# TensorE in a hardware loop of four packs, 16 heads' weights at a time, and V in 2 KB rows: two attention blocks on one core

**Chip, cores, metric.** One core of a Trainium2 chip. The metric is the device time of one execution in microseconds, lower is better. The four runs of the kernel before lie within 0.3% of each other (823.37 to 825.63 us).

## The reference

Two independent blocks A and B, the outputs joined along the last axis:

```python
B, Sq, D = 16, 64, 640          # batches, queries, width
H, Sk, Dh = 32, 512, 128        # heads, keys, head width
q = (x @ wq).reshape(B, Sq, H, Dh).transpose(0, 2, 1, 3)
scores = einsum("bhqd,bhkd->bhqk", q, k_cache) * Dh ** -0.5
p = softmax(scores, axis=-1)
o = einsum("bhqk,bhkd->bhqd", p, v_cache)
out = o.transpose(0, 2, 1, 3).reshape(B, Sq, H * Dh) @ wo      # all bf16
```

K and V are 67 MB each per block; about 292 MB must be loaded in all.

## The kernel before

The unit of work is a *pack*: four heads of two batches (2 x 64 queries fill the 128 rows). There are 128 packs. A planner lists the operations of every engine in order, finds which semaphores each must wait for, and the emitter writes all of it out, one instruction after the other. Per pack:

- TensorE: Q projection QP (20 matmuls), scores S (32 matmuls in 32x64 tiles), transposes of the normalised weights TR (2 x 8), PV (2 x 16), output projection OP (8). Each matmul comes with a weight load, so two instructions.
- VectorE: transposes K (KT, twice 1.24 us), evicts Q (QE) and the transposes (TE), reciprocals (RC).
- ScalarE: four exponentials (EX), two evictions of PV (OE). GpSimd: four normalisations (NM), and the reordering of a 512-column piece of wq (WP, 2.5 us) when a block begins.
- SyncE: all loads, in a planned order, into rings of buffers.

The parts that the change touches:

```python
def em_LDV(e, op):                    # V: 1 KB per descriptor
    src = blocks[blk][2][2 * bp + b, 4 * j:4 * j + 4].rearrange("g (p t) d -> p g t d", p=128)
    ...
def em_PV(e, op):                     # per pair of heads
    for s in range(2):
        for b in range(2):
            for t in range(4):
                col = s * 128 + 64 * b
                last = e.matmul(o_ps[:, col:col + 64], v_ring[:, n % NV, b, 2 * a + s, t, :],
                                pT_ring[:, m % NT, s, t, 64 * b:64 * b + 64], start=(t == 0), stop=(t == 3))
def em_OP(e, op):                     # per pair of heads; summed in PSUM over all 32 heads
    for s in range(2):
        h = (2 * m + s) % H
        last = e.matmul(out_ps0, oT_ring[:, m % NO, s, :], wo_sb[:, h, 0:N0], start=(h == 0), stop=(h == H - 1))
        ...                           # and the last 128 of 640 columns into out_ps1
def run_program(e, eng, p):
    for op in progs[eng]:             # every engine, TensorE too, is written out
        ...                           # waits, the instructions, the semaphore increment
```

## Time and profile before

| | before |
|---|---|
| time, median of 4 runs | 824.13 us |
| first scores / start of pack 8 / scores of the last pack | 12.1 / 91.1 / 805.9 us |
| mean pack from pack 8 on | 6.007 us |
| shortest pack | 5.30 us |
| 16 KB packets on the instruction queue | 112 |
| load rate in the steady stretches | 375 GB/s |

The lines of the page, of the two steady windows, of one hole and of the start stand in the prediction. A "pack" in the table is the time from one pack's first score matmul to the next one's. From pack 8 to the end the time is 119 x 6.007 us plus a tail, so whatever changes the mean pack by 0.1 us changes the total by 12 us.

### The profile page before, as it was taken

What the parts mean: (1) busy time and instruction counts of PE and PEld (TensorE: products, weight loads), DVE (VectorE), ACT (ScalarE), POOL (GpSimd) and SP (SyncE); (2) the same over time, 40 slices, a digit from 0 to 9 for tenths busy, and PEclk for the clock granted to TensorE, in tenths of its full rate; (3) what the DMA queues carried; (4) which work ended last, traced back from release to release, by engine and by line L of the source; (5) the groups of instructions that cost most, each with busy time, mean ns of one, the idle gap of its engine ahead of it and who ended that gap; (6) DMA issues with size and microseconds to landing.
All of it is one profiled execution on the core that took longest, in us unless ns stands there. A gap on an engine that the chain in (4) does not pass through costs nothing.

```text
span 824.6 us, 31476 instructions
## 1 busy us (share of the span) xinstructions
PE 707.0 (86%) x13777; PEld 521.7 (63%) x13905; DVE 578.7 (70%) x902; ACT 419.6 (51%) x1313; POOL 388.2 (47%) x550
## 2 busy tenths in 40 slices
PE   3069999999999999998778989999999999999994
PEld 2046776767666767676556666666666666666773
DVE  3047787777777787777556767777777777787773
ACT  2025655555554645554444555555555464555552
POOL 2068444444444444445665444444454444454442
PEclk9999999999999999999999999999999999999997
DMA  9999999999999999999999999999999999999980
GB/s 329 364 372 367 377 378 376 378 373 379 373 374 376 371 380 375 373 375 370 339 319 377 372 378 377 376 376 376 376 375 373 377 373 376 375 374 376 377 284 13
DMA packets 195729, 296.79 MB, mean 360 GB/s; under 512 B 9216, under 2 KB 162816, under 8 KB 195584
## 3 DMA queue, kind: packets, MB, share of 16 engines
q1 hardware_dynamic: 193280, 292.06, 100.2%
q8 instruction: 112, 1.84, 0.9%
q10 hardware_dynamic: 2304, 2.62, 0.9%
q14 instruction: 33, 0.27, 0.1%
HBM read 292.03 MB, written 2.62 MB: 357 GB/s over the span
## 4 chain that ended last, share of the span: by engine, by line
PE 70%; DMA 10%; SPq 6%; issue 6%; POOL 5%; DVE 3%; ACT 0%; ACTq 0%
PE ps L380 15%; PE ps L403 14%; PE ps L462 14%; PE ps L446 12%; PE ps L476 9%; DMA v_ring<-in_B_v_cache_dram 8%; PE ps L479 5%; DMA ws_ring<-in_A_wq_dram 2%; SPq L349 2%; SPq L342 2%; DVE kt_ring L393 2%; POOL pn_ring L438 2%; POOL wqp_sb L356 1%; POOL wqp_sb L357 1%; SPq L335 1%
## 5 line engine op out<-in xcount | busy, mean ns | idle before, releaser
L438 POOL TENSOR_SCALAR pn_ring<-p_ring,recip 128x512 bf16<-128x512 bf16 x512 | 349.2, 694 | 382.0 <-DVE recip L433 382.0
L418 ACT ACTIVATE p_ring<-ps 128x512 bf16<-128x512 f32 x512 | 304.2, 597 | 262.2 <-PE ps L403 262.2
L393 DVE STREAM_TRANSPOSE kt_ring<-kn_ring 128x1024 f32<-128x1024 f32 x256 | 316.0, 1235 | 7.6 <-DMA kn_ring<-in_A_k_cache_dram 7.5
L451 DVE COPY pT_ring<-ps 128x1024 bf16<-128x1024 bf16 x256 | 177.1, 692 | 161.3 <-PE ps L446 161.3
L446 PE MATMUL ps<-ident,pn_ring 128*128 128x128 bf16 x2048 | 158.0, 220 | 48.0 <-POOL pn_ring L438 46.8
L462 PEld LDWEIGHTS ps<-pT_ring,v_ring 128*128 128x128 bf16 x4096 | 141.5, 98 | 80.1 <-issue 64.7
L462 PE MATMUL ps<-pT_ring,v_ring 128*128 128x64 bf16 x4096 | 168.6, 194 | 21.8 <-issue 11.4
L380 PE MATMUL ps<-xT_ring,wqp_sb 128*128 128x128 bf16 x2560 | 169.7, 222 | 11.4 <-issue 9.1
L403 PE MATMUL ps<-kt_ring,qs_ring 32*64 32x512 bf16 x4096 | 155.2, 398 | 15.5 <-issue 13.4
L446 PEld LDWEIGHTS ps<-ident,pn_ring 128*128 128x128 bf16 x2048 | 122.4, 98 | 64.3 <-POOL pn_ring L438 49.1
L380 PEld LDWEIGHTS ps<-xT_ring,wqp_sb 128*128 128x128 bf16 x2560 | 153.1, 114 | 14.7 <-issue 11.4
L468 ACT ACTIVATE oT_ring<-ps 128x256 bf16<-128x256 f32 x256 | 98.5, 385 | 117.6 <-PE ps L462 117.4
L476 PE MATMUL ps<-wo_sb,oT_ring 128*128 128x512 bf16 x384 | 132.9, 387 | 0.1
L386 DVE TENSOR_SCALAR qs_ring<-ps 128x512 bf16<-128x512 f32 x128 | 88.6, 692 | 60.7 <-PE ps L380 60.7
L479 PE MATMUL ps<-wo_sb,oT_ring 128*128 128x128 bf16 x512 | 113.0, 221 | 8.2 <-issue 1.7
L418 ACT ACTIVATION_READ_ACCUMULATOR p_ring<-ps 128x1 f32 x512 | 105.6, 206 | 0.0
L403 PEld LDWEIGHTS ps<-kt_ring,qs_ring 32*64 32x64 bf16 x4096 | 57.1, 104 | 63.1 <-issue 24.4
L476 PEld LDWEIGHTS ps<-wo_sb,oT_ring 128*128 128x128 bf16 x512 | 50.3, 98 | 65.6 <-ACT oT_ring L468 33.3
L479 PEld LDWEIGHTS ps<-wo_sb,oT_ring 128*128 128x128 bf16 x512 | 50.7, 99 | 0.2 <-issue 0.2
L433 DVE RECIPROCAL recip<-rowsum 128x2 f32<-128x2 f32 x256 | 36.3, 142 | 6.6 <-ACT p_ring L418 6.4
L356 POOL COPY wqp_sb<-ws_ring 128x1280 bf16<-128x1280 bf16 x16 | 20.0, 1253 | 41.4 <-DMA ws_ring<-in_A_wq_dram 41.4
L357 POOL COPY wqp_sb<-ws_ring 128x1280 bf16<-128x1280 bf16 x16 | 20.1, 1256 | 0.0
(19 smaller groups left out, 39.5 us busy)
## 6 DMA issues: line engine op xcount, KB each, us to landing
kn_ring<-in_A_k_cache_dram SPq DMA_DIRECT2D x128, 512.0 KB, 10.2
v_ring<-in_A_v_cache_dram SPq DMA_DIRECT2D x128, 512.0 KB, 10.7
kn_ring<-in_B_k_cache_dram SPq DMA_DIRECT2D x128, 512.0 KB, 10.2
v_ring<-in_B_v_cache_dram SPq DMA_DIRECT2D x128, 512.0 KB, 10.7
ws_ring<-in_A_wq_dram SPq DMA_DIRECT2D x8, 640.0 KB, 9.4
wo_sb<-in_A_wo_dram SPq DMA_DIRECT2D x8, 640.0 KB, 10.6
ws_ring<-in_B_wq_dram SPq DMA_DIRECT2D x8, 640.0 KB, 8.3
wo_sb<-in_B_wo_dram SPq DMA_DIRECT2D x8, 640.0 KB, 11.2
```

Of the source, the lines that this page charges most:

```text
L380: last = e.matmul(ps[:, 0, f * 128:(f + 1) * 128], w[:, kt, f, :], xT_ring[:, xs, kt, :], start=(kt == 0), stop=(kt == KT - 1))
L386: ins = e.tensor_scalar(qs_ring[:, op.idx % NQ].rearrange("p f b q -> p (f b q)"), ps[:, 0, :], scale, None, ALU.mult)
L393: ins = e.transpose(dst, kn_ring[:, n % NK, b, :].bitcast(F32))
L403: last = e.matmul(ps[64 * b:64 * b + 64, i, :], qs_ring[rows, n % NQ, f, b, :], kt_ring[rows, n % NKT, b, :, f // 2, :, f % 2], start=(f = ...
L418: ins = e.activation(dst, src, ACTF.Exp, scale=1.0, accum_out=rowsum[:, h:h + 1])
L438: ins = e.tensor_scalar(pn_ring[:, h % NPN, :], p_ring[:, h % NP, :], recip[:, (h // 2) % NR, h % 2:h % 2 + 1], 1.0, ALU.mult, ALU.mult)
L446: last = e.transpose(pt_ps[:, s, t, :], pn_ring[:, h % NPN, t * 128:(t + 1) * 128], ident[:, :])
L451: ins = e.tensor_copy(pT_ring[:, op.idx % NT].rearrange("p s t q -> p (s t q)"), pt_flat)
L462: last = e.matmul(o_ps[:, col:col + 64], v_ring[:, n % NV, b, 2 * a + s, t, :], pT_ring[:, m % NT, s, t, 64 * b:64 * b + 64], start=(t == ...
L468: ins = e.activation(oT_ring[:, op.idx % NO].rearrange("p s q -> p (s q)"), o_ps, ACTF.Copy)
L476: last = e.matmul(out_ps0, oT_ring[:, m % NO, s, :], wo_sb[:, h, 0:N0], start=(h == 0), stop=(h == H - 1))
L479: last = e.matmul(out_ps1, oT_ring[:, m % NO, s, :], wo_sb[:, h, N0:D], start=(h == 0), stop=(h == H - 1))
```

## The change

Its intent: TensorE's program is turned into a hardware loop, so that its instructions need not be fetched again and again. A *turn* is one pass through the loop body. The body is written once, so its addresses and wait values are the same in every pass. So buffers and weights must repeat with the body (NJ = PERIOD = NV = 4 packs, thus 16 heads' weights in SBUF at a time instead of 32), the output sums of the two halves of the heads are added in SBUF, and every semaphore that TensorE waits for is lowered at the end of a turn by what a turn added. V comes in rows of 2 KB; a partition then holds eight keys in a row, a head takes 64 partitions, and PV becomes pairs of matmuls over half the rows, in two row tiles of the array.

```diff
-    NK = 5   NV = 5   NWS = 2   NP = 4   NPN = 4   NO = 2          (condensed)
+    NK = 7   NV = 4   NWS = 4   NP = 2   NPN = 2   NO = 1   PERIOD = 4   FIRST = 3
-            src = blocks[blk][2][2 * bp + b, 4 * j:4 * j + 4].rearrange("g (p t) d -> p g t d", p=128)
+            src = blocks[blk][2][2 * bp + b, h:h + 4].rearrange("(a s) (p t) d -> (s p) a (t d)", s=2, t=8)
@@ em_PV: once a pack
-            for s in range(2):
+            for a in range(2):
                 for b in range(2):
-                    for t in range(4):
-                        last = e.matmul(o_ps[:, col:col + 64], v_ring[:, n % NV, b, 2 * a + s, t, :], ...)
+                    for t in range(8):
+                        for s in range(2):
+                            rows = slice(64 * s, 64 * s + 64)
+                            last = e.matmul(o_ps[:, s, col:col + 64], v_ring[rows, n % NV, b, a, t, :],
+                                            pT_ring[rows, (2 * n + a) % NT, t, 64 * b:64 * b + 64],
+                                            start=(t == 0), stop=(t == 7), tile_position=(64 * s, 0))
@@ em_OP: once a pack, a pack later; new em_OA, em_OV add the sums into acc on VectorE
@@ run_program, for TensorE
+            with e.Fori(0, reps):
+                for op in prog[lo:lo + size]:
+                    emit(e, op, p, {})
+                for s, v in sorted(per.items(), key=str):
+                    e.sem_inc(sems[p][s], -v * units(s))
```

Cut: the planner's checks that the waits are periodic, the replacement of waits that would not be, new order times, and the exponential's and the transposes' addressing.

## The prediction

> **What bounds the kernel now.** I read the page first, then the windows by stage, then the order of time inside single packs, then the waits, and last the trace's packet records. A pack is four heads of two batches: 1 MB of K, 1 MB of V; there are 128 of them. From the page:

> ```profile
> span 824.6 us, 31476 instructions
> PE 707.0 (86%) x13777; PEld 521.7 (63%) x13905; DVE 578.7 (70%) x902; ACT 419.6 (51%) x1313; POOL 388.2 (47%) x550
> ...
> PE   3069999999999999998778989999999999999994
> ...
> DMA  9999999999999999999999999999999999999980
> GB/s 329 364 372 367 377 378 376 378 373 379 373 374 376 371 380 375 373 375 370 339 319 377 372 378 377 376 376 376 376 375 373 377 373 376 375 374 376 377 284 13
> ...
> q1 hardware_dynamic: 193280, 292.06, 100.2%
> q8 instruction: 112, 1.84, 0.9%
> ```

> Two things are full at once. TensorE is at 9 in nearly every slice, except the first three and slices 19 to 23, where new weights come in. The DMA engines are at 9 from the first slice to the 38th, and their rate never passes 380 GB/s. The windows of the two steady stretches say the same (columns: length, busy time of PE, PEld, DVE, ACT, POOL with counts, clock, DMA share, GB/s):

> ```profile
> 110.00:390.00 280.00, 259.60 (x5121) 192.09 (x5165) 214.65 (x334) 156.28 (x492) 131.93 (x192) 1.00 1.06 375
> 444.00:780.00 336.00, 307.56 (x6102) 227.21 (x6155) 255.04 (x397) 184.68 (x580) 154.06 (x226) 1.00 1.06 375
> ```

> Which leads? Taking pack starts (first score matmul of each pack) from the trace, a pack lasts 5.31 us when nothing disturbs TensorE, and that exact value comes back again and again (packs 12, 30, 36, 48, 51, 108). The mean between packs 66 and 120 is (767.0 - 444.7) / 54 = 5.97 us. The difference is holes like this one (PE rows in order of time; the bracket is idle time and what ended it):

> ```profile
> 239.09 0.72 PE L380 MATMUL ps<-xT_ring,wqp_sb 128*128 128x128 bf16 x10
> 241.19 0.75 PE L380 MATMUL ps<-xT_ring,wqp_sb 128*128 128x128 bf16 x10 [1.38 <-issue]
> ```

> The hole splits one run of identical matmuls, so no data is missing: the instructions are. The queue of instruction fetches has 112 packets of 16 KB, one for every 256 TensorE instructions, and one starts at 238.71 us, just before this hole. So **instruction fetch** costs TensorE some 0.5 to 0.6 us a pack. Behind it stands the DMA. V of packs 72 to 84 lands within 0.1 us of its first use; by pack 126 it is 7.6 us early. The loads thus gain only about 7.6 / 42 = 0.18 us a pack on TensorE: DMA-limited period about 5.75 us, TensorE about 5.95.

> The start is lost too. From the chain of waits:

> ```profile
> 35.49 9.42 DMA ws_ring<-in_A_wq_dram
> 44.96 1.26 POOL wqp_sb L356
> 46.22 1.20 POOL wqp_sb L357
> ```

> TensorE starts at 12 us, then waits until 49 us for a slice of wq that sits in the queue behind 30 us of other loads, because the two staging slots had to come free first.

> [...]whether a loop stays resident no run here shows yet. [...]packets of 1,024 bytes take 49.6 ns, of 4,096 bytes 168.5 ns, not four times as much. [...]Here scores (32x64 tiles) issue matmuls 3 to 4 ns apart in groups of eight, and the change from transposes to scores costs 149 ns start to start instead of 56, that from scores to PV 314 instead of 213: some 95 ns each.

> **The change, part by part.**

> *TensorE per pack, from 5.31 us.* Scores (1.07), transposes (8 at 56 ns, twice, 0.90) and the Q projection (20 at 56 ns, 1.12) stay. PV had 32 matmuls at 29 ns, 0.94 us; now it has 64 with half the rows, two row tiles at a time. If two tiles run side by side, as the scores do, 32 pairs at 29 ns are 0.94 us again. PV now needs a tiling mode of its own: two more mode changes, +0.19. The output projection had 4 x (0.215 + 0.056) = 1.08 us plus a wait of 0.265 us for the second head pair's eviction (321 ns start to start where 56 would do; "ACT oT_ring L468" ends 33.3 us of such waits). It now starts a pack later on one eviction for all four heads: -0.265. Sum 5.24 us.

> *Instruction fetch.* The loop body is 4 x (20 + 32 + 16 + 64 + 8) + 5 = 565 matmuls, two instructions each, 1,130, with waits and a dozen semaphore decrements about 1,150[...]. The choice of 16 heads, which makes addresses repeat after four packs, only makes sense if this fits; eight packs would be 2,260. I take it that it stays resident: the 0.6 us holes go[...]. TensorE period about 5.4 us. 31 turns of the loop: 124 x 0.5 = 62 us off TensorE's path.

> *DMA.* Sum of packet times over 16 engines before: 1,024-byte packets 141,312 x 49.6 ns / 16 = 438 us, 1,280-byte loads 38, 4,096-byte 345, stores 7, instructions 8, semaphores and tables 7: 842 us in a window of about 798 us (the page's 1.06: packets overlap a little). A line through the two sizes gives 2,048 bytes 89.2 ns. V's 131,072 packets become 65,536: 406 -> 365 us, -41. Instruction fetch falls by about 7. x is loaded once more for each half of the heads, +2,048 packets of 1,280 bytes, +7.6. New sum 801, times 798/842: 760 us. If the overlap is a constant 3.9 ns per packet instead, a V packet of each size loses that, V gives only 25 us, and the window is 773. I take 765. This is what the change is worth per pack: 5.75 -> about 5.5.

> *Other engines.* VectorE gets the partial sums[...]. ScalarE loses 16 output copies and does one eviction of 512 in place of two of 256. GpSimd's weight copies are the same 32 at 1.25 us, now four up front and four at each of three changes; with them a pack needs 2.5 + 4 x 0.694 = 5.3 us of GpSimd, close to the period, where eight packs before took 7.6 us each.

> *Start and end.* Four staging slots and only four wq slices: all are requested before anything can block them, so the stop until 49 us shrinks to a few us. This gives TensorE about 30 us, but it gives the DMA nothing, since that worked through the stop at 364 to 372 GB/s.

> So TensorE needs about 15 + 128 x 5.4 + 10 for changes of weights + 15 = 730 us, the DMA 2 + 765 + the work after the last V. Before, 22 us passed after it because TensorE lagged; now PV, eviction, output projection, sum, store and the closing check remain, estimate 13 us. **The bound moves from TensorE with its instruction fetch to the DMA: 2 + 765 + 13 = 780 us, 5.3% less.**

> **Rivals.**
> 1. *The loop does not stay resident.* Then 1,150 instructions are 4.5 fetches in four packs (1.1 a pack against 0.85), plus a stall of some 3 us at each turn (the last two fetches of the trace, around the closing jump, are 3.1 us apart). TensorE: 5.24 + 0.65 + 0.75 = 6.6 us a pack, total about 880.[...]
> 2. *The row tiles do not overlap.* 64 matmuls at 29 ns are 1.88 us; period about 6.3 us, 31 + 128 x 6.3 = about 835. For it: weight loads of 128 columns come 29 ns apart, no closer, in the PV of now. Against it: the scores' loads go 3 to 4 ns apart in different tiles. At a half-way cost the DMA would still hide it.
> 3. *A chain of latencies sets the period.* Scores, four exponentials and one eviction (about 3.9 us), reciprocal, two normalisations (1.4), transpose: about 6.6 us from a pack's scores to its second transpose, which stands only one pack later in TensorE's order. It closes at about 5.4 us a pack, so it hides under the DMA; with VectorE's added work in the way it could make 5.8: 790.
> 4. *2 KB rows bring nothing*, if the memory and not the packet overhead sets 376 GB/s. Then the DMA stays at 798: total 812, within 2%.

> **Range and chances.** With a resident loop, tilings that overlap and a saturated DMA, the two readings of the overlap give 775 to 788; a better ordered start and end or a larger effect of the packet size allow 757, a latency chain or rival 4 up to 812. I put 10% on rivals 1 and 2 together. Faster by over 2% (below 807): 0.85; within: 0.07; slower: 0.08.

> **What would show it.** Right: the instruction queue falls from 112 packets to about 20; "issue" disappears from TensorE's waits inside packs; DMA share stays at 9 throughout, now at 388 to 395 GB/s; 2,048-byte packets near 89 ns; V lands just before use, and waits for V and K become TensorE's and VectorE's largest. PV about 1 us a pack with gaps of about 0.1 us around it. Wrong: instruction packets over 100, holes of microseconds every four packs, PV matmuls 29 ns apart without pairs, or a DMA below 9 in steady packs, which would put the bound on a chain of engines.

That the body of about 1,150 instructions stays resident was an assumption. One term of TensorE's sum is cut, an estimate for the decrements and the branch at the turn; with it the sum came to about 5.4 us a pack and 730 us in all. The two durations and the sum for VectorE's new work are cut too (it came to 81% busy); in the changed kernel an addition of 128x128 takes 0.28 us, one of 128x512 0.67 us, and VectorE is busy for 78%. The 780 us are the DMA's sum, 2 + 765 + 13, and lose no term. The 13 us for the end and the 10 us for changes of weights are estimates.

## The result

792.4 us (median of 4 runs, 791.67 to 792.93) against 824.13. The ratio is 0.9612 [0.9594, 0.963]. Here and below a ratio is the mean time of one kernel's fast runs over that of the other's fast runs of the same rounds, so not quite the ratio of the medians.

The page of the changed kernel, its lines that answer to those of before:

```profile
span 790.7 us, 40216 instructions
PE 706.0 (89%) x17953; PEld 533.3 (67%) x18081; DVE 616.3 (78%) x1062; ACT 406.8 (51%) x1185; POOL 386.8 (49%) x550
...
PE   4668999999999999999999999999999999999994
...
DMA  9999999999999999999999999999999999999950
GB/s 319 388 396 397 396 393 396 393 394 384 396 385 397 391 377 393 390 388 370 382 392 393 398 397 397 398 396 390 383 389 387 396 399 397 400 398 399 399 215 15
...
q8 instruction: 11, 0.18, 0.1%
```

112 instruction packets became 11, and none of them lies between 74.3 and 774.4 us: the loop stays resident. The loads run up to 400 GB/s. The dips of slices 19 to 24 in TensorE's row are gone. But both rows are still full, and the page does not say which of the two leads. The waits do, all that are over 10 us and end idle time of TensorE (engine, line, what it waited for: total us, times, longest us):

```profile
PEld ps L562 <- PEq L724: 45.3, 31, 1.5
PEld ps L604 <- DVE pT_ring L610: 42.6, 95, 1.5
PE ps L562 <- PEq L724: 39.9, 31, 1.3
PEld ps L522 <- issue: 30.0, 32, 10.8
PE ps L522 <- DMA xn_ring<-in_A_x_dram: 16.4, 2, 10.3
```

There is no line for V or K. The second line is idle time of the weight loads alone, and the matmul row of the same instructions has 1.3 us: scores were running. "PEq" is TensorE's own sequencer and L724 is the row of semaphore decrements at the end of the loop body. 31 turns wait there for 39.9 us. In order of time, TensorE's rows around one turn:

```profile
117.08 1.11 PE L622 MATMUL ps<-pT_ring,v_ring 64*128 64x64 bf16 x64
118.12 0.62 PE L604 MATMUL ps<-ident,pn_ring 128*128 128x128 bf16 x8
120.02 1.14 PE L562 MATMUL ps<-kt_ring,qs_ring 32*64 32x512 bf16 x32 [1.28 <-PEq L724]
```

The trace's own records show why: the twelve decrements start 0.151 us apart, 1.81 us in all, then 0.10 us for the loop counter and 0.27 us for the branch (its record lasts 212 ns). The transposes queued before them cover only part of that.

So from pack 8 on TensorE never waits for loaded data. The packs repeat in fours: 5.41, 5.41, 6.77 (the turn), 5.70 us (the pack with the five transposes of x). The mean is 5.41 + (1.36 + 0.28) / 4 = 5.82 us, and 5.824 is what the starts give. V lands at least 2.0 us ahead of its use in every pack from 9 on. K's lead is below 0.3 us only in packs 101 to 103, after the last change of weights, and no pack there is longer than its fellows.

Where the 33.9 us of the two spans went:

| stretch | before | after | difference |
|---|---|---|---|
| to the start of pack 8 | 91.1 | 79.1 | -12.0 |
| 119 packs to the last | 119 x 6.007 = 714.8 | 119 x 5.824 = 693.1 | -21.8 |
| after the last pack's first scores | 18.6 | 18.5 | -0.1 |

The differences are those of the unrounded times. The middle line is a difference of larger terms. Gone are the fetch holes (714.8 less 119 x 5.31, less about 14 us at the change of block and 4 us of x transposes: about 65 us, of which 8 us were waits for V, over 103 fetches) and the slow change of block. Added are 30 turns at 1.36 us (41 us), 0.10 us a pack (12 us) and twice as many x transposes (4 us).

### The profile page after: what moved, and what is told of

Its sections match the earlier page's. It is cut to its first block, busy times and chain, and to the rows that moved or that the text cites. A ratio compares the mean times of both kernels' runs of the same rounds, so it can differ in the third digit from the quotient of the medians.

```text
span 790.7 us, 40216 instructions
## 1 busy us (share of the span) xinstructions
PE 706.0 (89%) x17953; PEld 533.3 (67%) x18081; DVE 616.3 (78%) x1062; ACT 406.8 (51%) x1185; POOL 386.8 (49%) x550
## 4 chain that ended last, share of the span: by engine, by line
PE 60%; PEld 14%; issue 10%; DVE 8%; SPq 4%; DMA 1%; PEldq 1%; ACT 0%; DVEq 0%
PE ps L562 13%; PE ps L604 12%; PE ps L539 11%; PE ps L622 11%; PE ps L638 8%; PE ps L641 5%; PEld ps L539 5%; PEld ps L622 4%; PEld ps L604 3%; DVE pT_ring L610 3%; SPq L501 2%; DVE kt_ring L552 2%; PE ps L522 2%; DMA xn_ring<-in_A_x_dram 1%; PEld ps L638 1%
## 5 line engine op out<-in xcount | busy, mean ns | idle before, releaser
L577 ACT ACTIVATE p_ring<-ps 128x512 bf16<-128x512 f32 x512 | 298.9, 599 | 189.2 <-PE ps L562 189.2
L610 DVE COPY pT_ring<-ps 128x1024 bf16<-128x1024 bf16 x256 | 173.2, 677 | 118.4 <-PE ps L604 117.8
L562 PE MATMUL ps<-kt_ring,qs_ring 32*64 32x512 bf16 x4096 | 147.1, 398 | 46.5 <-PEq L724 39.9
L629 ACT ACTIVATE oT_ring<-ps 128x512 bf16<-128x512 f32 x128 | 76.4, 597 | 170.5 <-PE ps L622 170.5
L604 PEld LDWEIGHTS ps<-ident,pn_ring 128*128 128x128 bf16 x2048 | 117.3, 98 | 50.5 <-DVE pT_ring L610 42.6
L622 PE MATMUL ps<-pT_ring,v_ring 64*128 64x64 bf16 x8192 | 142.3, 190 | 2.9 <-issue 2.2
L622 PEld LDWEIGHTS ps<-pT_ring,v_ring 64*128 64x128 bf16 x8192 | 126.8, 95 | 15.1 <-issue 2.5
L638 PE MATMUL ps<-wo_sb,oT_ring 128*128 128x512 bf16 x384 | 118.8, 381 | 0.0
L651 DVE TENSOR_TENSOR acc<-acc,ps 128x128 f32<-128x128 f32 x96 | 27.0, 281 | 10.9 <-PE ps L641 2.1
L528 ACT ACTIVATE xT_ring<-ps 128x640 bf16<-128x640 bf16 x32 | 22.3, 696 | 15.0 <-PE ps L522 15.0
```

The costliest lines, as they stand in the source:

```text
L562: last = e.matmul(ps[64 * b:64 * b + 64, i, :], qs_ring[rows, n % NQ, f, b, :], kt_ring[rows, n % NKT, b, :, f // 2, :, f % 2], start=(f = ...
L577: ins = e.activation(dst, src, ACTF.Exp, scale=1.0, accum_out=rowsum[:, h:h + 1])
L604: last = e.transpose(pt_ps[:, t, :], pn_ring[:, op.idx % NPN, t].rearrange("q s k -> q (s k)"), ident[:, :])
L610: ins = e.tensor_copy(pT_ring[:, op.idx % NT].rearrange("p t q -> p (t q)"), pt_flat)
L622: last = e.matmul(o_ps[:, s, col:col + 64], v_ring[rows, n % NV, b, a, t, :], pT_ring[rows, (2 * n + a) % NT, t, 64 * b:64 * b + 64], star ...
L629: ins = e.activation(oT_ring[:, op.idx % NO].rearrange("p s a q -> p s (a q)"), o_ps, ACTF.Copy)
```

## The experiments

**Theory:** the changed kernel is bound by TensorE, through the row of decrements at the turn, with the DMA some ten microseconds behind; the loop pays because its body stays resident. **Rivals:** the DMA already sets the time; or it is the branch that costs.

Ten kernels ran in three batches, each timed in three rounds against the kernel before (medians 825.1, 824.5 and 825.9 us). All gave correct results.

**1. Decrements spread over the body.**

```diff
+            last = {s: i for i, op in enumerate(body) for s, _ in op.waits}
             with e.Fori(0, reps):
-                for op in prog[lo:lo + size]:
+                for i, op in enumerate(body):
                     emit(e, op, p, {})
-                for s, v in sorted(per.items(), key=str):
-                    e.sem_inc(sems[p][s], -v * units(s))
+                    for s, v in sorted(per.items(), key=str):
+                        if last[s] == i:
+                            e.sem_inc(sems[p][s], -v * units(s))
```

> The same loop with its twelve semaphore decrements no longer in one row at the end, but each straight after the last wait of the loop body that uses its semaphore. Theory (the decrements cost 0.151 us each in TensorE's sequencer and, standing together, outlast the queued matmuls): the fourth pack start of each turn falls from 6.77 us to 5.4 to 5.8 us, the idle time put down to TensorE's sequencer at the loop's end falls from 39.9 us to under 12 us, and TensorE's path gets 31 to 42 us shorter. Then the DMA becomes the bound at 297.8 MB / 396 GB/s = 752 us plus about 20 us of start and end: total 768 to 778 us. Rival (the turn's 1.35 us are the branch and the drain of the queue, whatever stands before it): the fourth pack stays at 6.6 to 6.8 us and the total at 788 to 793 us.

Measured 781.52 us, ratio 0.9478 [0.944, 0.9516], the fastest kernel of this study. The turn is gone: the median pack with the turn lasts 5.42 us. But the mean pack is 5.740 us, not 5.48, because now data are missing. The views of waits, changed kernel and then this one (the eviction of Q, `qs_ring`, follows the transposes of K in VectorE's order, so a late K shows at TensorE as a wait for it):

```profile
DVE kt_ring L552 <- DMA kn_ring<-in_A_k_cache_dram: 15.8, 4, 10.1
```

```profile
DVE kt_ring L552 <- DMA kn_ring<-in_B_k_cache_dram: 33.0, 31, 3.4
PEld ps L562 <- DVE qs_ring L545: 31.7, 22, 3.2
...
DVE kt_ring L552 <- DMA kn_ring<-in_A_k_cache_dram: 19.4, 10, 10.0
```

K lands less than 0.3 us before its use in about 60 packs from 9 on. The loss isn't spread evenly: packs 53 to 68 and 91 to 101, around which new weights are loaded beside K and V, take 29 of the 31 us by which the 119 packs exceed TensorE's own 5.41 and 5.69 us; the others run at TensorE's pace. The loads themselves never pause until their end (DMA share 1.04 to 1.05 in the stretches from 80 to 700 us), so TensorE paces ordinary packs and the sum of the loads sets the total. The 41 us taken off TensorE's path brought 11: the DMA took over. Its floor is about 781 us, a little over the 768 to 778 that I expected. The branch as the cause has fallen.

**2. Twelve more decrements.**

```diff
+                for _ in range(6):
+                    e.sem_inc(s_fl, 1)
+                    e.sem_inc(s_fl, -1)
```

> The changed kernel with twelve more semaphore operations at the end of the loop body, on a semaphore that nobody waits for (six times plus one, minus one). Theory (each costs 0.151 us in the sequencer, nothing hides these): a turn gets 12 x 0.151 = 1.81 us longer, the fourth pack 8.5 to 8.7 us, the total 31 x 1.81 = 56 us longer, 843 to 850 us. Rival (branch and drain cost, the decrements are free): total 790 to 800 us.

Measured 883.71 us, 91 us longer, not 56. The pack with the turn lasts 8.63 us, 1.86 longer than 6.77: the theory's 1.81 for each turn. The other 35 us have another cause. The next pack lasts 5.70 us in some turns and 7.3 in others. TensorE's rows around a turn of the second kind, first the output projection before it, then the turn, then the output projection after it:

```profile
410.97 0.38 PE L638 MATMUL ps<-wo_sb,oT_ring 128*128 128x512 bf16 x1
411.19 0.22 PE L641 MATMUL ps<-wo_sb,oT_ring 128*128 128x128 bf16 x1
...
418.05 1.13 PE L562 MATMUL ps<-kt_ring,qs_ring 32*64 32x512 bf16 x32 [3.12 <-issue]
...
420.11 0.63 PE L638 MATMUL ps<-wo_sb,oT_ring 128*128 128x512 bf16 x1
420.54 0.31 PE L641 MATMUL ps<-wo_sb,oT_ring 128*128 128x128 bf16 x1
```

After the hole of 3.1 us the same matmul takes 0.63 us in place of 0.38. The trace's clock records hold 20 windows of 3.413 us at half speed between 129 and 843 us, and one of twice that length at 75 us; the changed kernel has none between 51 and 788 us. 22 x 3.413 / 2 = 38 us at most; the mean granted clock is 0.946 against the changed kernel's 0.987. With 31 x 1.81 = 56 that makes 94, against 91 measured. So most of these holes of 3.1 us cost clock as well as their own length. Some shorter holes did too. In the kernel before, around the window at 395.6 us:

```profile
389.59 0.38 PE L476 MATMUL ps<-wo_sb,oT_ring 128*128 128x512 bf16 x1
...
394.20 0.62 PE L446 MATMUL ps<-ident,pn_ring 128*128 128x128 bf16 x8 [2.09 <-POOL pn_ring L438]
...
397.34 0.63 PE L476 MATMUL ps<-wo_sb,oT_ring 128*128 128x512 bf16 x1
```

The hole of 2.1 us at 430 us there has such a window after it too (at 433.1 us), and five holes of 1.9 to 2.4 us in experiment 5; others of that length have none, such as those of 2.1 us that end at 409.7 and 417.3 us in the kernel before. The changed kernel's turns, with holes of up to 1.3 us, never do.

**3. TensorE written out, the rest as changed.**

```diff
-            if eng != "pe":
+            if True:
                 for op in prog:
                     emit(e, op, p, {})
                 return
```

> The changed kernel without the loop: TensorE's program written out, all else the same. Theory (instruction fetch was the first thing on the path, and the loop is what removed it): 141 or more instruction packets of 16 KB instead of 11, holes put down to issue of 0.5 to 0.7 us each are back, the loop's 42 us are saved; total 815 to 840 us, slower than the changed kernel. Rival (the kernel before was bound by the DMA, its holes were hidden, and the loop brings nothing): total 765 to 792 us.

Measured 880.16 us, ratio 1.0693 to the kernel before, with these packets on the instruction queue:

```profile
q8 instruction: 144, 2.36, 1.1%
```

The loop is worth 88 us here. The total lies outside both expectations, since the holes were longer than I thought: the mean pack is 6.54 us, 1.06 above 5.41 and the x transposes, for 1.1 fetches a pack, so about 0.95 us a fetch (a part of it clock windows at half speed, 8 of them after the start; the mean granted clock is 0.970).

**4. A body of eight packs.**

```diff
-    PERIOD = 4
+    PERIOD = 8
```

> The changed kernel with a loop of eight packs in place of four: about 2,290 instructions in the body in place of about 1,145, 15 turns in place of 31 and four packs more outside. Theory (the loop pays only because its body fits TensorE's instruction memory[...], and the run with twelve more instructions still fitted): the body is fetched anew at each turn, 125 to 150 instruction packets in place of 11, the holes of the written-out run are back, total 850 to 890 us. Rival (what stays resident is larger than 2,290 instructions, or only the branch target matters): 10 to 45 instruction packets, half as many turns, total 775 to 790 us.

Measured 1000.82 us, far outside what I expected. The instruction queue and the longest hole of one stretch:

```profile
q8 instruction: 160, 2.62, 1.0%
```

```profile
288.56 1.93 PE L562 MATMUL ps<-kt_ring,qs_ring 32*64 32x512 bf16 x32 [9.59 <-issue]
```

160 packets in place of 11: the body of about 2,290 instructions is not kept. The first scores of a pack wait up to 10.2 us for "issue" (143.2 us in 43 such waits); the one above stands at a turn, and I read it as a jump to code that has to be fetched first. The mean granted clock is 0.919. This loop is worse than none: 1000.8 us against 880.2 for TensorE written out.

**5 and 6. V in 1 KB rows again, with the loop as changed and with spread decrements.**

```diff
-            src = ....rearrange("(a s) (p t) d -> (s p) a (t d)", s=2, t=8)
+            src = ....rearrange("g (p t) d -> p g t d", p=128)
@@ em_PV: 32 matmuls over 128 rows in place of 64 over 64 (EX, NM and TR address alike)
```

> The changed kernel with V in 1 KB rows again, and PV again as 32 matmuls over 128 rows; loop, sums in SBUF and 16 heads at a time stay. TensorE's pack loses two changes of tiling mode, 5.42 to about 5.24 us. Theory (the changed kernel is bound by TensorE, but the DMA is close behind, and the 2 KB rows are what keeps it behind): V's packets cost 406 us of the 16 engines instead of 362, the DMA becomes the bound, V lands less than 1 us before its use, and the total is 800 to 815 us. Rival (the DMA had room enough without the longer rows): TensorE's shorter pack shows, total 765 to 775 us.

> Spread decrements, and V in 1 KB rows with PV over 128 rows. Theory (with 1 KB rows the DMA is the bound, at about 815 us, whatever TensorE's loop costs): 808 to 818 us, less than 10 us under the same kernel with the decrements in a row (818.0), though TensorE's path is 42 us shorter; V in 2 KB rows is then worth 27 to 37 us as soon as TensorE is out of the way. Rival (the loop's turn was still on the path there): 776 to 800 us.

Measured 817.95 us with the decrements in a row and 816.72 us with them spread, the first a little above its range. TensorE's shortest pack falls to 5.20 us, yet the total rises by 26 and 35 us. The waits of the first:

```profile
DVE kt_ring L552 <- DMA kn_ring<-in_B_k_cache_dram: 48.1, 53, 2.7
```

K arrives just in time (less than 0.3 us ahead) in some 70 packs, and 41 us less work at the turns change 1 us. With 1 KB rows the DMA is the bound, at 817; with 2 KB rows it is at 781. The rows are worth 35 us once the turn is hidden; without them the loop brought 7 us against the kernel before in the same rounds, and 8 with the turn hidden.

**7. Neither loop nor 2 KB rows.**

> The changed kernel with neither the loop nor the 2 KB rows: TensorE written out, V in 1 KB rows, PV in 32 matmuls; 16 heads at a time and the sums in SBUF stay. Theory (the written-out run with 2 KB rows fell to 880 us because PV in halves raises TensorE's instructions per pack from about 220 to 283, so it fetches more often): about 110 instruction packets in place of 144, TensorE's pack 5.3 plus 0.86 x 0.7 = 5.9 us, DMA floor 817, total 815 to 835 us, near the kernel before. Rival (the 16-heads arrangement itself costs, without the loop): 850 to 890 us.

Measured 823.17 us, ratio 0.9976 [0.9944, 1.0007] to the kernel before, with 112 instruction packets. So 16 heads at a time, sums in SBUF and the new order, taken together, neither gain nor lose in the total; no run separates them, and their parts differ (pack 8 starts 15 us earlier than in the kernel before, the mean pack is 6.11 us against 6.01). The fetches hardly show here: TensorE's matmuls are idle for 6 us on "issue" in all, against 96 us in experiment 3, because K is late in some 77 packs and TensorE waits for it anyway. Together with 3 and 5 this makes a square:

| | V in 1 KB rows | V in 2 KB rows |
|---|---|---|
| TensorE written out | 823 | 880 |
| loop, decrements in a row | 818 | 792 |
| loop, decrements spread | 817 | 782 |

The longer rows alone lose 57 us: PV in halves raises the fetches from 112 to 144, and TensorE then waits for them instead of for K; the loop alone gains 5; both together gain 31.

**8. x of the second group of packs earlier.**

```diff
-        loads.append((txt - 0.1, ..., 0, op))
+        loads.append((txt - 0.1, ..., 0, op) if g != 1 else (-6.0, -5.0, 0, op))
```

> The changed kernel with the load of the second group's x moved nine places forward in the load queue (it holds up TensorE from about 34 to 46 us). Theory (TensorE bounds the changed kernel, so time lost at its start is lost for good): the pack of 18.1 us at the start falls to 7 to 12 us, total 780 to 788 us. Rival (the DMA sets the time): total within 2 us of the changed kernel, 790 to 794 us.

> Spread decrements and the early x together. Theory (with spread decrements the DMA is the bound, so an earlier start of TensorE brings almost nothing more): 777 to 782 us, against 781.5 with spread decrements alone. Rival (TensorE still bounds most of the run): 770 to 775 us.

Measured 790.34 us alone, above what I expected and in the rival's range, and 781.63 us with spread decrements, as expected. In the first, pack 8 starts at 72.1 us, 7.0 us ahead of the changed kernel's 79.1, and pack 64 is still 7.0 us ahead; pack 96 is 4.5 ahead, the last one 2.2. The lead is lost after packs 64 and 96, where new weights are loaded beside K and V. So "bound by TensorE" is too simple: TensorE sets the pace of ordinary packs, and a kernel that runs ahead meets the DMA at the changes of weights.

**9. PV's row halves one after the other.**

```diff
-                    for t in range(8):
-                        for s in range(2):
+                    for s in range(2):
+                        for t in range(8):
```

> The changed kernel with the same 64 PV matmuls in another order: first the eight of one row half, then the eight of the other, in place of alternating halves. Theory (alternating is what lets two row tiles work side by side, a pair in 29 ns): PV's matmuls come 29 ns apart one by one, PV takes about 1.9 us in place of 0.94, the pack about 6.35 us, total 792 + 128 x 0.94 = about 912 us (890 to 925). Rival (TensorE pulls the other half's work ahead by itself): 788 to 800 us.

Measured 820.38 us, between the two expectations. PV's rows in the changed kernel, then here (start to the start of the transposes that follow is its length):

```profile
117.08 1.11 PE L622 MATMUL ps<-pT_ring,v_ring 64*128 64x64 bf16 x64
118.12 0.62 PE L604 MATMUL ps<-ident,pn_ring 128*128 128x128 bf16 x8
```

```profile
119.91 1.35 PE L622 MATMUL ps<-pT_ring,v_ring 64*128 64x64 bf16 x64
121.19 0.62 PE L604 MATMUL ps<-ident,pn_ring 128*128 128x128 bf16 x8
```

PV takes 1.28 us in place of 1.04, not 1.9. 64 matmuls at 29 ns one after the other would take 1.86 us, so part of the work still overlaps; which part, this view does not show. In the changed kernel the two matmuls of a pair start 3 to 4 ns apart, one pair every 29 ns. The order is worth 0.24 us a pack, 28 us in all.

## Why the prediction came close, and where it was wrong

*The total* was 780 us with a range of 757 to 812; it is 792.4.

*What bounded the kernel before.* The prediction had TensorE 0.18 us a pack behind the DMA, which is 23 us over 128 packs. Experiment 6 says less. There the fetches and the turn are off TensorE's path and V still comes in 1 KB rows, and the last V lands at 800.2 us against 802.1 in the kernel before. Of the 800.2, about 7 us are the second load of x there (2,048 packets of 59 ns over 16 engines). So TensorE held the loads up by some 9 us, an estimate: loads and fetches bounded the kernel before almost equally.

*That the fetches vanish*: right, 11 packets (I said about 20).

*"The bound moves from TensorE with its instruction fetch to the DMA"*: wrong for this kernel. V lands 2 us or more before its use, and spreading the decrements brings 11 us. The step that failed is the term for the decrements and the branch, an estimate that rested on no trace. They cost 1.36 us at a turn: twelve times 0.151 us, the counter (0.10) and the branch (0.27), less what the queue covers. Over 31 turns that is 27 us more than the sum had.

*TensorE's pack*: 5.24 predicted, 5.41 measured. The mis-sized term is the wait for the second eviction, 0.265 us, which I had taken from a single pack with a disturbance. An ordinary pack of the kernel before:

```profile
305.88 0.22 PE L479 MATMUL ps<-wo_sb,oT_ring 128*128 128x128 bf16 x1
306.03 0.39 PE L476 MATMUL ps<-wo_sb,oT_ring 128*128 128x512 bf16 x1
```

The second starts 0.15 us after the first where 0.056 would do: 0.095 us of wait. 5.31 + 0.19 - 0.095 = 5.405, which is the measured pack. That also agrees with the 0.19 us for two more changes of tiling mode (start to start, projection to PV takes 152 ns in the changed kernel and 56 before, PV to transposes 123 and 29) and the 29 ns for a pair of PV matmuls; experiment 5, without these changes of mode, has a pack of 5.20 us, 0.21 less. The idle times of 33.3 us that I quoted were those of the weight loads, 0.27 us each, and a weight load is idle for about 0.12 us of that between two 512-column matmuls anyway.

*The DMA*: 2,048-byte packets were to take 89.2 ns and take 88.4; the sum was to be 801 us and is 791. The floor of 780 us that I put on the whole kernel is what the kernel with spread decrements shows, 781.5. So the number 780 was right for a kernel in which the turn is hidden, and 11 of the 12 us of error are the turn; the longer pack alone, which that kernel has too, costs nothing there. In part 780 was luck. With spread decrements the packet times sum to 789 us and fill a window of 762: the sum was 12 us too high, and the packets overlap by 1.035 and not by 842/798 = 1.055, so the two errors nearly cancel (765 predicted). And the 3.9 ns per packet of the other reading come to 3.6 from the prediction's own figures, which moves its 773 us by about 1.

*The start*: TensorE was to gain about 30 us. Pack 8 starts 12 us earlier. The wait for wq is gone, but another took its place, the load of x for the second group, 10.3 us at 46 us (moving it gives 7).

*Rivals*: rival 1, a body that is not kept, was put at about 880; with eight packs it is 1000.8, because the holes are longer than the 3 us it assumed (up to 10.2) and the clock falls too (0.919). Rival 2, tiles that do not overlap, is excluded by the 3 to 4 ns. Rival 3, a chain of latencies, was put at 790 us and 5.8 us a pack, which is close to the 792.4 and 5.82 measured, but by chance: experiment 1 leaves that chain as it is, and the turn's pack falls from 6.77 to 5.42 us. Rival 4, rows that bring nothing, is excluded by the square; its 812 us, for a DMA that stays as slow as before, is near the 817 of experiments 5 and 6.

**Still open:** why a fetch costs more in the written-out kernel with 2 KB rows (about 0.95 us) than before (about 0.55, its waits for V left out). Its denser instructions may leave less queued work to cover the fetch; no run tests that alone. And what remains of the start, 79.1 us for eight packs, was not taken apart further.
